# Combination weights turned by four small products, and results stored by transfers that span all 128 partitions

## The chip, the cores and the metric

The kernel runs on one core of one Trainium2 chip. The metric is device time in microseconds (us), the median of several executions. The profile is that of one execution, taken by the hardware profiler. Its engines are TensorE (PE, with its weight loads as PEld), VectorE (DVE), ScalarE (ACT), GpSimd (POOL) and SyncE (SP). SP issues every DMA of this kernel, all on one queue.

## The reference

Eight batches of 576 rows go through attention in chunks of 64 rows, over 8 heads of 64. The result is a matrix x of 4608 rows (tokens) by 512. A soft mixture of experts follows: every token has logits against 32 slots (8 experts with 4 slots each); a softmax over all tokens (`d`) makes the slots' inputs, each expert runs its two matrices on its 4 slots, and a softmax over the 32 slots (`c`) mixes the slots' outputs back into tokens.

```python
# attention, chunk = 64
attn = softmax(scale * q_c @ k_c.T)          # within each chunk of 64 rows
out = attn @ v_c
x = out.transpose(0, 2, 1, 3).reshape(B * S, H * D)       # 4608 x 512
# mixture of experts
logits = x @ phi                             # 4608 x 32
d = softmax(logits, axis=0)
slot_input = (d.T @ x).reshape(E, S_per_e, D)
slot_out[e] = np.maximum(slot_input[e] @ w1[e], 0.0) @ w2[e]
c = softmax(logits, axis=1)
return c @ slot_out                          # 4608 x 512
```

Everything is float32.

## The kernel before

**Tiles of tokens.** The kernel works on nine groups of 512 tokens (index `b`, list `batch`). Eight groups are the first 512 rows of one batch each; the fifth group, at position 4 of the list, collects the last 64 rows of all eight batches. A group is cut into 8 chunks of 64 tokens. Within a group each of four head pairs makes one step, so attention has 36 steps `t`, software pipelined in the loop of lines 427 to 460: `s1` scores, `s2a` transposed weights, `s2b` the product with v, `s3` the transposed x (`xT`), and every fourth step the logits and softmax parts of an earlier group.

**Where a token stands.** `s2b` writes chunk `4m + 2*r2 + c2` (for a normal group: tokens `256m + 128*r2 + 64*c2 + q`, with q from 0 to 63) to partitions `64m + q` of the tile `xb`, at indices `c2` and `r2` of its free dimensions. `s3` (line 261) and `products` (line 361) take the four slices of `xb` that span 128 partitions as `j`, with `c2 = j % 2` and `r2 = j // 2`. One slice thus holds 64 tokens of the group's first half on partitions 0 to 63 and 64 tokens of its second half on partitions 64 to 127.

**Combination weights.** `combination` (lines 338 to 346) leaves the weights `c` of a group in `c_all`, 128 partitions (token within the slice) by 4 slices by 32 slots, the last step being a multiplication on GpSimd. `turn_c` (lines 99 to 103) turns this 128 x 128 block by one TensorE transpose into PSUM and a ScalarE copy back, so that partitions `32j` to `32j+31` hold the 32 slots of slice `j` and the columns its 128 tokens. It is called by `place` for seven groups in the attention loop (at t = 9, 13, ... 33, after `s2a` and before `s1b` and `s2b`), and twice in line 635, between the last `up` of the experts and the last `turn`.

**Weights from memory.** After attention the 16 w1 and 16 w2 blocks of 1 MB each are loaded into the pools `wpa`, `wpb` and the old q/k tiles as these come free (`load_w`, `refill`). All loads have 128 partitions and stand on SP's queue ahead of the stores.

**The last stage.** `down(e, h)` accumulates half h (256 of the 512 columns) of the slots' outputs, `gather` and `spread` copy them to all four row quarters, and `combine(b, h)` (lines 608 to 627) makes the result of group b, half h. For each of the four row quarters one product of 32 rows (`cc[rs]`) gives 128 tokens by 256 columns. Two quarters stand in one PSUM pair and are copied by ScalarE (i = 0) and VectorE (i = 1) into `ob`, 128 partitions by 4 by 256. Then line 627 issues two transfers, one for partitions 0 to 63 and one for 64 to 127: each is 64 partitions by 4 pieces of 1 KB, 256 KB. Two, because the tokens of the upper 64 partitions are not those that follow the lower ones in memory. The order written out by hand in line 643 interleaves the nine `combine(b, 0)` with `down(e, 1)`; the loop of lines 646 and 647 makes the nine `combine(b, 1)`. The tiles `ob` come from the pools of the weights and are separate for each group.

Of the kernel before, what the change touches and what calls it, by code (L numbers as in the profile page):

```python
# [16 lines left out]
def kernel(  # L17
# [10 lines left out]
    nc = tc.nc  # L28
# [3 lines left out]
    B, H, S, D = q.shape  # L32
    P = 128
    CH = 64
# [5 lines left out]
    BT = 4 * P  # L40
# [16 lines left out]
    batch = [0, 1, 2, 3, B] + list(range(4, B))  # L57
# [4 lines left out]
    ident = const.tile([P, P], F32, name="ident")  # L62
# [35 lines left out]

    def turn_c(b, pc):

        cc = c_all[:, 4 * b:4 * b + 4, :].rearrange("p j s -> p (j s)")
        nc.tensor.transpose(out=pc[:, 0:P], in_=cc, identity=ident)
        nc.scalar.copy(cc, pc[:, 0:P])

    with ExitStack() as actx:
# [5 lines left out]
        def bank(name):  # L111
            return ps.tile([P, 512], F32, tag="ps", name=name)

        def pair(name):
            return psp.tile([P, 2, 512], F32, tag="psp", name=name)
# [9 lines left out]
        def tiles(name, shape, which):  # L125
            return {i: ap_.tile([P] + shape, F32, name=f"{name}{i}") for i in which}
# [5 lines left out]
        xb = tiles("x", [2, NHP, 2, P], [1])  # L132
# [124 lines left out]
        def s3(t):  # L257
            px = bank(f"px_{t}")
            n, hp = divmod(t, NHP)
            for j in range(4):  # L260
                nc.tensor.transpose(  # L261
                    out=px[:, P * j:P * (j + 1)], in_=xb[n % 2][:, j % 2, hp, j // 2], identity=ident)
            pv = px.rearrange("p (j x) -> p j x", j=4)
            o = xT[:, :, hp]
            if t == NT - 1 or t % 2 == 0 and t < NT - 6:
                nc.vector.tensor_copy(o, pv)  # L266
            else:
                nc.scalar.copy(o, pv)
# [81 lines left out]
        def partial(b):  # L350
            products(b)
            accumulate(b)

        def products(b):
            eN = lst[b][0]
            pp = pps[b] = bank(f"pp_{b}")
            for j in range(4):
                nc.tensor.matmul(
                    pp[SL * j:SL * (j + 1), :],
                    lhsT=eN[:, j, :],  # L360
                    rhs=xb[b % 2][:, j % 2, :, j // 2],
                    start=True, stop=True,
                )

# [9 lines left out]
        def place(b):  # L374
            turn_c(b, bank(f"pc_{b}"))
# [51 lines left out]
        for t in range(NT - 2):  # L427
# [20 lines left out]
            if t >= 3:  # L448
                s3(t - 3)
# [16 lines left out]
        s1b(t - 1)  # L466
        s1(t)
        s3(t - 4)
        s2b(t - 3)
        load_v(t)  # L470
# [5 lines left out]
        s2b(t - 2)  # L476
        s2a(t)
        s3(t - 3)
        s2b(t - 1)
        natural(NL - 2, False)  # L480
        s2b(t)
        s3(t - 2)
        products(NL - 2)
        s3(t - 1)
        s3(t)
# [122 lines left out]
    def combine(b, h):  # L608
        if h == 0:
            obs[b] = (wpa if b < 7 else wpb).tile([P, 2048], F32, tag="w", name=f"ob_{b}")  # L610
        ob = obs[b].rearrange("p (h j f) -> p h j f", h=2, j=4)[:, h]
        cc = c_all[:, 4 * b:4 * b + 4, :].rearrange("p j s -> p (j s)")
        for i in range(2):
            pf = pair(f"pf_{h}_{b}_{i}")
            for j in range(2):
                rs = slice(SL * (2 * i + j), SL * (2 * i + j + 1))
                nc.tensor.matmul(pf[:, j, 0:DH], lhsT=cc[rs], rhs=sst[h][rs], start=True, stop=True)  # L617
            copy = nc.scalar.copy if i == 0 else nc.vector.tensor_copy
            copy(ob[:, 2 * i:2 * i + 2], pf[:, :, 0:DH])  # L619
        ov = out.rearrange("(b s) f -> b s f", s=S)[..., DH * h:DH * (h + 1)]  # L620
        for x in range(2):

            if batch[b] < B:
                o = ov[batch[b], 4 * CH * x:4 * CH * (x + 1)].rearrange("(j q) f -> q j f", j=4)
            else:
                o = ov[4 * x:4 * x + 4, BT:S].rearrange("j q f -> q j f")
            nc.sync.dma_start(o, ob[CH * x:CH * (x + 1)])

    hrs = {}
    for e in range(0, E, 2):  # L630
# [3 lines left out]
    for b in (NL - 2, NL - 1):  # L634
        turn_c(b, bank(f"pc_{b}"))
# [4 lines left out]


    steps = {"d": lambda e: down(e, 1), "c": lambda b: combine(b, 0), "g": gather, "s": spread}
    order = "s0 d0 c0 c1 d1 c2 d2 c3 d3 c4 d4 c5 d5 c6 d6 c7 d7 g1 c8 s1"
    for x in order.split():
        steps[x[0]](int(x[1:]))
    for b in range(NL):
        combine(b, 1)
# [30 lines left out]
```

## Time and profile before

| | |
|---|---|
| time, median of 3 runs | 256.41 us (256.22 to 256.86) |
| time of the profiled execution | 255.84 us |
| its span in the trace | 254.0 us |
| mean granted TensorE clock | 0.968 |
| PE busy | 214.0 us (84%) |
| DVE busy | 158.7 us (63%) |
| ACT busy | 144.4 us (57%) |
| POOL busy | 6.8 us (3%) |
| bytes read from and written to memory | 61.93 MB, 9.44 MB |
| packets of the one DMA queue | 89168, 98.0% of 16 engines' span |

The span is the time from the first to the last event that the trace shows; the execution takes 1.8 us more. The profile's page cuts the span into 40 slices of 6.35 us and gives for each how busy the engines were, in tenths. The chain of waits follows the work that ended last back from the end. Other views give, for one source line, the durations of its instructions (lowest, median, highest, in ns) and the time from a DMA's issue to its landing (in us), or, for stretches of time, the busy time of the engines and what the DMA engines moved.

### The profile page before, as it was taken

Reading aid. Unit: us, or ns where it says so; the run is one execution under the profiler, and the core shown is the slowest. Engines: PE = TensorE matmul, PEld = TensorE weight load, DVE = VectorE, ACT = ScalarE, POOL = GpSimd, SP = SyncE. Lnnn points to the kernel's source line nnn. Section 1 sums busy time; section 2 is a strip of 40 time slices with the busy share of each in tenths; the row PEclk is TensorE's granted clock in tenths of the full one; section 3 lists DMA queues with packets and bytes.
Section 4 is the critical chain, followed back from the end, with each engine's and each line's share of the span. In section 5 each row is a group of like instructions: output and inputs, shape, how many; then the busy total and the mean of one; then the engine's idle time right before and its main releaser. Section 6 shows DMA issues by size and latency. Waiting matters only on the chain.

```text
span 254.0 us, 7973 instructions
## 1 busy us (share of the span) xinstructions
PE 214.0 (84%) x3262; PEld 150.0 (59%) x3262; DVE 158.7 (63%) x356; ACT 144.4 (57%) x291; POOL 6.8 (3%) x29
## 2 busy tenths in 40 slices
PE   6888988998998998998998998989899998988000
PEld 3667876875885785875776776676533453445000
DVE  4578786986985985985985985985630102456100
ACT  2697868758758757867767776775221202345000
POOL 1000000000000000000000000000040000000000
PEclk9999999999999999999999999999999999999755
DMA  6999999999999899999999788986999999999996
GB/s 193 335 293 268 318 337 295 277 273 244 257 269 199 264 317 243 308 322 341 290 308 300 217 242 227 354 215 230 320 331 346 348 348 347 321 254 258 275 254 183
DMA packets 89203, 71.88 MB, mean 283 GB/s; under 512 B 41040, under 2 KB 85072, under 8 KB 89168
## 3 DMA queue, kind: packets, MB, share of 16 engines
q1 hardware_dynamic: 89168, 71.38, 98.0%
q8 instruction: 26, 0.43, 0.7%
q14 instruction: 9, 0.07, 0.1%
HBM read 61.93 MB, written 9.44 MB: 281 GB/s over the span
## 4 chain that ended last, share of the span: by engine, by line
PE 46%; DVE 22%; ACT 19%; issue 4%; DMA 1%; POOL 0%; ACTq 0%; DVEq 0%
ACT qkT L188 15%; PE pqk L173 7%; PE po L583 6%; DVE qkT L186 6%; PE psc L200 6%; PE ph L551 6%; DVE x L250 5%; PE pav L241 5%; PE px L261 4%; PE pf L617 4%; PE pt L223 3%; DVE xT L266 3%; DVE sc L210 2%; DVE mx L208 1%; DVE rc L249 1%
## 5 line engine op out<-in xcount | busy, mean ns | idle before, releaser
L188 ACT COPY qkT<-pqk 64x512 f32<-64x512 f32 x107 | 66.7, 624 | 29.8 <-PE pqk L173 28.1
L173 PE MATMUL pqk<-ident,qk_w 128*128 128x128 f32 x288 | 40.4, 284 | 5.4 <-DVE qkT L186 4.7
L186 DVE COPY qkT<-pqk 64x512 f32<-64x512 f32 x37 | 25.8, 696 | 23.3 <-ACT qkT L188 19.8
L200 PE MATMUL psc<-qkT 128*64 128x128 f32 x576 | 39.4, 279 | 1.0 <-DVE qkT L186 1.0
L173 PEld LDWEIGHTS pqk<-ident,qk_w 128*128 128x128 f32 x288 | 31.6, 143 | 14.3 <-DVE qkT L186 7.0
L200 PEld LDWEIGHTS psc<-qkT 128*64 128x64 f32 x576 | 30.7, 137 | 4.0 <-ACT qkT L188 1.2
L261 PE MATMUL px<-ident,x 128*128 128x128 f32 x144 | 22.7, 282 | 5.6 <-DVE x L250 4.9
L210 DVE TENSOR_TENSOR sc<-psc,mx 128x512 f32<-128x512 f32 x36 | 24.9, 691 | 1.3
L250 DVE TENSOR_TENSOR x<-pav,rc 128x512 f32<-128x512 f32 x36 | 24.9, 691 | 1.2
L261 PEld LDWEIGHTS px<-ident,x 128*128 128x128 f32 x144 | 15.6, 141 | 16.6 <-DVE x L250 11.8
L241 PE MATMUL pav<-v,at 64*64 64x65 f32 x1152 | 25.1, 224 | 0.3 <-ACT eN L324 0.3
L208 DVE TENSOR_REDUCE mx<-psc 128x8 f32<-128x512 f32 x36 | 24.4, 677 | 0.5 <-PE psc L200 0.4
L223 PE MATMUL pt<-ident,sc 128*128 128x128 f32 x144 | 22.1, 275 | 2.8 <-ACT sc L215 1.6
L241 PEld LDWEIGHTS pav<-v,at 64*64 64x64 f32 x1152 | 20.1, 134 | 5.8 <-issue 3.7
L215 ACT ACTIVATE sc<-sc 128x512 f32<-128x512 f32 x36 | 23.1, 642 | 0.1
L225 ACT COPY at<-pt 128x512 f32<-128x512 f32 x36 | 21.2, 588 | 1.9 <-PE pt L223 1.5
L619 DVE COPY ob<-pf 128x512 f32<-128x512 f32 x18 | 12.2, 689 | 12.7 <-PE pf L617 12.7
L223 PEld LDWEIGHTS pt<-ident,sc 128*128 128x128 f32 x144 | 16.6, 141 | 3.9 <-ACT sc L215 2.3
L619 ACT COPY ob<-pf 128x512 f32<-128x512 f32 x18 | 10.3, 586 | 13.0 <-PE pf L617 12.0
L617 PE MATMUL pf<-sst,c_all 32*128 32x256 f32 x144 | 14.3, 423 | 1.6 <-ACT ob L619 0.5
L551 PE MATMUL ph<-w,siT 128*32 128x512 f32 x128 | 14.6, 596 | 0.1
L583 PE MATMUL po<-w,hz 128*32 128x256 f32 x224 | 14.3, 383 | 0.1
(86 smaller groups left out, 172.9 us busy)
## 6 DMA issues: line engine op xcount, KB each, us to landing
w<-in_moe_w_dram SPq DMA_DIRECT2D x30, 1024.0 KB, 7.3
out_dram<-ob SPq DMA_DIRECT2D x36, 256.0 KB, 4.3
qk_w<-in_k_dram SPq DMA_DIRECT2D x32, 256.0 KB, 5.7
qk_w<-in_q_dram SPq DMA_DIRECT2D x32, 256.0 KB, 5.8
v<-in_v_dram SPq DMA_DIRECT2D x64, 128.0 KB, 5.0
qk_w<-in_moe_w_dram SPq DMA_DIRECT2D x2, 1024.0 KB, 7.6
qk_w<-in_k_dram SPq DMA_DIRECT2D x8, 128.0 KB, 5.5
qk_w<-in_q_dram SPq DMA_DIRECT2D x8, 128.0 KB, 5.2
```

What stands on the lines that cost most here:

```text
L173: nc.tensor.transpose(out=pt[:, 1 - isq, o:o + P], in_=src[:, a, P * i:P * (i + 1)], identity=ident)
L186: nc.vector.tensor_copy(o, pv[D * j:D * (j + 1), a])
L188: nc.scalar.copy(o, pv[D * j:D * (j + 1), a])
L200: nc.tensor.matmul(pv[CH * r2:CH * (r2 + 1), m, c2], lhsT=qT[:, o:o + CH], rhs=kb[:, :, o:o + CH], start=True, stop=True,)
L208: nc.vector.reduce_max(mx, pv, axis=AX.X)
L210: nc.vector.tensor_tensor(sc.rearrange("p (r x) -> p r x", x=CH), pv, mx.unsqueeze(2).to_broadcast([P, 8, CH]), ALU.subtract)
L223: nc.tensor.transpose(out=pt[:, P * r:P * (r + 1)], in_=sc[:, r], identity=ident)
L241: nc.tensor.matmul(pav[CH * m:CH * (m + 1), c2, i * VW:(i + 1) * VW], lhsT=at[rs, 2 * m + a, r2, :], rhs=v_sb[t % NV][rs, 2 * m + r2, a, : ...
L250: nc.vector.tensor_tensor(xb[n % 2][:, :, hp].rearrange("p c m (a d) -> p c (m a) d", a=2), av[..., 0:D], rc.to_broadcast([P, 2, 4, D]), A ...
L261: nc.tensor.transpose(out=px[:, P * j:P * (j + 1)], in_=xb[n % 2][:, j % 2, hp, j // 2], identity=ident)
L551: nc.tensor.matmul(ph[SL * i:SL * (i + 1), :], lhsT=siT[:, j, :], rhs=wt[1, e, j // 2][:, j % 2, DM * h:DM * (h + 1)], start=(j == 0), sto ...
L583: nc.tensor.matmul(po[h][SL * c:SL * (c + 1), :], lhsT=hzs[e][:, 2 * c + b, :], rhs=w[:, 2 * c + b, :], start=(e == 0 and b == 0), stop=(e ...
```

## The change

```diff
     def turn_c(b, pc):
         cc = c_all[:, 4 * b:4 * b + 4, :].rearrange("p j s -> p (j s)")
-        nc.tensor.transpose(out=pc[:, 0:P], in_=cc, identity=ident)
+        for c2 in range(2):
+            for x in range(2):
+                rs = slice(CH * x, CH * (x + 1))
+                nc.tensor.matmul(pc[rs, CH * c2:CH * (c2 + 1)], lhsT=cc[rs, CH * c2:CH * (c2 + 1)],
+                                 rhs=ident[rs, rs], start=True, stop=True)
         nc.scalar.copy(cc, pc[:, 0:P])
...
-                    out=px[:, P * j:P * (j + 1)], in_=xb[n % 2][:, j % 2, hp, j // 2], identity=ident)
+                    out=px[:, P * j:P * (j + 1)], in_=xb[n % 2][:, j // 2, hp, j % 2], identity=ident)
...
-                    rhs=xb[b % 2][:, j % 2, :, j // 2],
+                    rhs=xb[b % 2][:, j // 2, :, j % 2],
...
-        for x in range(2):
-
-            if batch[b] < B:
-                o = ov[batch[b], 4 * CH * x:4 * CH * (x + 1)].rearrange("(j q) f -> q j f", j=4)
-            else:
-                o = ov[4 * x:4 * x + 4, BT:S].rearrange("j q f -> q j f")
-            nc.sync.dma_start(o, ob[CH * x:CH * (x + 1)])
+        if batch[b] < B:
+            nc.sync.dma_start(ov[batch[b], 0:BT].rearrange("(j p) f -> p j f", j=4), ob)
+        else:
+            for c2 in range(2):
+                nc.sync.dma_start(ov[c2::2, BT:S].rearrange("j q f -> q j f"), ob[CH * c2:CH * (c2 + 1)])
```

The slices `j` are numbered the other way (`c2 = j // 2`, `r2 = j % 2`). `turn_c` makes four products of a 64 x 64 block with a 64 x 64 identity in place of the transpose of the whole block: each 64 x 64 block is turned, and it stays in its half of the partitions, while a transpose of the whole moves the two off-diagonal blocks across. The row quarter `2x + j % 2` then holds 128 tokens that follow each other, `128 * quarter + column`. So in a normal group the partitions of `ob` are tokens in the order of memory, and `combine` stores its 512 KB by one transfer of 128 partitions by 4 pieces of 1 KB. The collected group, whose chunks come from eight batches, is still stored by two transfers of 64 partitions. In place of 36 transfers of 256 KB there are 16 of 512 KB and 4 of 256 KB.

## The prediction

> **What bounds the kernel now.** I read the page's slices first, for where the compute engines stop.
>
> ```profile
> span 254.0 us, 7973 instructions
> ...
> PE   6888988998998998998998998989899998988000
> PEld 3667876875885785875776776676533453445000
> DVE  4578786986985985985985985985630102456100
> ACT  2697868758758757867767776775221202345000
> ...
> DMA  6999999999999899999999788986999999999996
> GB/s 193 335 293 268 318 337 295 277 273 244 257 269 199 264 317 243 308 322 341 290 308 300 217 242 227 354 215 230 320 331 346 348 348 347 321 254 258 275 254 183
> ```
>
> In the last three slices (19 us) no compute engine does anything, while the DMA engines are busy to the end. The chain of waits agrees: its last piece is a copy of the last results.
>
> ```profile
> 234.84 1.29 DVE ob L619 x2
> ```
>
> It ends at 236.1; the remaining 17.9 us are stores that are still flowing. So the second view is the busy time by stretches (columns: length; PE, PEld, DVE, ACT, POOL busy; granted clock, DMA share, GB/s).
>
> ```profile
> 208.00:214.00 6.00, 5.00 (x62) 2.46 (x54) 1.12 (x2) 1.41 (x3) 0.00 (x0) 1.00 1.09 348
> 216.00:218.00 2.00, 2.00 (x36) 0.92 (x36) 1.01 (x2) 0.94 (x2) 0.00 (x0) 1.00 1.07 342
> 218.00:220.00 2.00, 2.00 (x36) 0.84 (x28) 1.05 (x2) 0.80 (x2) 0.00 (x0) 1.00 1.06 341
> 220.00:222.00 2.00, 2.00 (x35) 0.92 (x32) 0.71 (x2) 0.59 (x1) 0.00 (x0) 1.00 0.95 283
> 222.00:226.00 4.00, 4.00 (x57) 1.80 (x56) 1.90 (x4) 1.32 (x3) 0.00 (x0) 1.00 0.93 258
> 226.00:236.00 10.00, 8.00 (x74) 4.40 (x73) 6.41 (x10) 5.98 (x11) 0.00 (x0) 1.00 0.93 261
> 236.00:246.00 10.00, 0.00 (x0) 0.00 (x0) 0.13 (x1) 0.00 (x0) 0.00 (x0) 0.59 0.92 260
> 246.00:252.00 6.00, 0.00 (x0) 0.00 (x0) 0.00 (x0) 0.00 (x0) 0.00 (x0) 0.50 0.89 255
> 252.00:254.00 2.00, 0.00 (x0) 0.00 (x0) 0.00 (x0) 0.00 (x0) 0.00 (x0) 0.50 0.09 29
> ```
>
> To 214 the queue carries weight loads of 128 partitions, at 348 GB/s. From 222 it carries stores alone, at 255 to 261, with the engines still 0.89 to 0.93 busy. Loads and stores both move pieces of 1 KB. So the bound from about 217 on is the store stream, and it runs at three quarters of the rate just shown by the same engines. From 220 to the end the rows add up to 2·283 + 4·258 + 10·261 + 10·260 + 6·255 + 2·29 = 8396 KB. At about 255 the last row holds 0.2 us of flow, so 8396 KB take 32.2 us, 261 GB/s.
>
> **Why it is slow.** The third view is that of the storing line and of the two lines that load v, the second of them for the collected group.
>
> ```profile
> L627 SPq DMA_DIRECT2D out_dram<-ob x36: 595/931/1307, 213.8 to 248.8; - x36
> ...
> DMA to landing us min/median/max: 3.7/4.3/5.5
> ...
> L162 SPq DMA_DIRECT2D v<-in_v_dram x16: 595/607/868, 72.5 to 92.8; - x16
> ...
> DMA to landing us min/median/max: 3.9/6.0/8.2
> ...
> L157 SPq DMA_DIRECT2D v<-in_v_dram x64: 367/458/1618, 2.8 to 165.9; - x64
> ...
> DMA to landing us min/median/max: 2.3/5.0/7.1
> ```
>
> Line 162 moves 64 KB to 64 partitions, line 157 128 KB to 128 partitions, in the same pieces. With half the bytes the 64-partition transfer costs SP more (595 against 367 ns at best) and lands later (3.9 against 2.3 us at best, 6.0 against 5.0 in the median). So transfers of half the partitions are the slow kind also as loads, and writing memory is not needed for it. (The comparison isn't clean: the sources of line 162 lie further apart.) The stores are this kind: their quickest issue takes the same 595 ns.
>
> [...]
>
> **The change, part by part.**
>
> *Stores.* 32 of the 36 transfers become 16 of 512 KB from 128 partitions; the collected group's 4 stay. Both halves waited for the same two copies before, so nothing is issued later than now. SP's 36 issues lie end to end (36.25 us from 213.8 to the end of the last):
>
> ```profile
> 203.83 5.71 SPq L95 DMA_DIRECT2D w<-in_moe_w_dram  x2
> 213.78 36.25 SPq L627 DMA_DIRECT2D out_dram<-ob  x36
> ```
>
> so either SP paces the stream or the engines push back on it; both ways are eased. 20 issues at the 931 ns median would be 18.6 us, at the 458 ns of line 157, which has as many pieces for each transfer, 9.2 us. Either is under the time the bytes need. If an issue grew with its pieces to 2 x 931 ns, SP would again set the pace: a rival below.
>
> The rate after isn't in the trace, since no store has 128 partitions. Lower bound: 255 GB/s, today's. Upper bound: short stretches of mixed loads run higher than 348, as the slices of the stretch from 72 to 95 us (0.575 us each) show:
>
> ```profile
> GB/s 130 100 349 335 378 328 386 362 304 175 131 183 181 249 221 183 86 194 138 147 55 126 21 406 370 385 435 344 372 347 249 231 210 306 378 370 374 372 378 315
> ```
>
> some 375 held for 3 us. I take 345, between the loads of 128 partitions in the same pieces (348) and the best stretch that is mostly stores (341). The 8396 KB take 24.3 us in place of 32.2: **-7.9 us**.
>
> *What is late next.* Would the results come in time? The copies of the first half end at about 213.7 and then every 1.64 us, to 226.6; the second half's first group ends at 228.5, the last at 236.1.
>
> ```profile
> 225.91 0.69 DVE L619 COPY ob<-pf 128x512 f32<-128x512 f32 x1 [0.18 <-PE pf L617]
> ...
> 227.70 1.07 ACT L619 COPY ob<-pf 128x512 f32<-128x512 f32 x2 [0.80 <-PE pf L617]
> 227.76 0.69 DVE L619 COPY ob<-pf 128x512 f32<-128x512 f32 x1 [1.16 <-PE pf L617]
> ```
>
> At 345 GB/s one 512 KB transfer takes 1.52 us. The stores begin to flow at 217.0: 9.44 MB of stores less 8.40 MB are 1.04 MB before 220, 3.0 us at 341. Then group k of the first half starts at 217.0 + 1.52k, the first of the second half at 230.7. Its copies end at 228.5; with some 2 us from issue to flow (an estimate: the 2.3 us best landing of line 157 less its own 0.4) it is there at 230.4, just in time. The end of 244.3 lies 8 us behind the last copy, so the queue stays the bound. Only much over 345 GB/s would the first half run dry: at 375 the second half starts at 230.4 and the nine end at 243.0, a gain of 9.2; without any limit of the queue the last copy's 236.1 and a landing of 3.7 give 239.8, a gain of 12.4.
>
> *Turning.* Nine transposes go, 36 products come. Row of the transposes, row of the products of this shape (64x64 against 65 columns), and one step's 32 of them:
>
> ```profile
> L102 PE MATMUL pc<-ident,c_all 128*128 128x128 f32 x9 | 2.9, 320 | 0.7 <-ACT hr L562 0.3
> ...
> L241 PE MATMUL pav<-v,at 64*64 64x65 f32 x1152 | 25.1, 224 | 0.3 <-ACT eN L324 0.3
> ...
> 48.38 0.70 PE L241 MATMUL pav<-v,at 64*64 64x65 f32 x32
> ```
>
> A float32 product leaves two records (16 products a step, 32 records), so a turn has 8. At best, overlapped as in line 241, they take 0.70·8/32 = 0.18 us, below the transpose's 0.32; in a row 8·0.224 = 1.79, 1.47 more. The nearest row is the overlapped one with a lead of one product, about 0.35 us. For the seven turns in attention, which no idle PE hides in full, and the two that stand ahead of `down`, I take +0.2 us in all; bounds -1.2 and +13.2. The copy behind it keeps its shape.
>
> *Numbering of the slices.* Lines 261 and 361 read the same shapes with the same partitions in another order: 0.
>
> **Sum.** On the profiled execution: 255.8 - 7.9 + 0.2 = 248.1 us. The median of the runs is 0.6 above the profiled one (256.4 against 255.8), so 256.4 - 7.7 = **248.7 us**. At 341 and 348 GB/s it is 249.0 and 248.5.
>
> **Rivals.**
>
> - *Half the way.* Another limit, such as memory's writing or the last halves of the collected group, holds the stream near 300 GB/s: 28.0 us in place of 32.2, 252.4. For it: 341 was seen for only some 4 us, with a backlog and the end of the loads beside it. Against: 341 is still a stretch in which most bytes are stores.
> - *No gain.* The store stream is limited by bytes or pieces written, not by its shape: 261 GB/s stay, 256.6 with the turns. A doubled issue (2 x 931 ns for 512 KB, 282 GB/s) would give 29.8 us and 254.2, near it. [...] Against it speak the rows of lines 157 and 162.
> - *Slower.* The four products run one behind the other where PE sets the pace, in the turn between transposes and line 241: 1.47 us each, 13.2 for nine, 256.4 - 7.9 + 13.2 = 261.7. It decides from 0.9 us a turn (7.9/9), and sooner if the stores gain less. Against it stands the row of 32 records in 0.70 us.
> - *It does not do what it says.* The bytes and the piece size (1 KB) stay; only if the transfer were spread over fewer engines than now would it fail; this would be the second rival's number or worse.
>
> **How the numbers follow.** Forecast (330 GB/s or more, 246 to 250 us): 0.66. Half the way (250 to 254): 0.17. No gain: 0.11, which is within 0.3%, about what a measurement of this kernel can tell from no change. Slower: 0.06. Faster 0.83, same 0.11, slower 0.06. Failing to do what it says is within no gain. The range begins at 246.0, between the 247.4 of 375 GB/s and the 244.2 of a queue without limit, and ends at 253.5 (some 275 to 280 GB/s); it leaves out the worst of half the way, no gain and slower, and holds 0.66 and some 0.14.
>
> **What would show it.** The GB/s of the stretches behind 220 rise to 330 or more; the span's end lies 8 to 9 us behind the last copy, not 18; issues of 512 KB take under 1.5 us of SP; copies end at 236 as now, a few tenths later if the turns cost; the group of the turn shows 8 records in some 0.35 us. Wrong would be: 260 GB/s again (no gain), or copies that end over 1 us later (turns on the path).

## The result and the profile after

| | before | changed |
|---|---|---|
| median | 256.63 us (256.22 to 257.39, 4 runs) | 249.18 us (249.11 to 250.24, 4 runs) |
| profiled execution: span | 254.0 us | 247.4 us |
| mean granted TensorE clock | 0.968 | 0.985 |

The ratio is 0.9716, 95% interval 0.968 to 0.9751: faster by 2.8%. The forecast was 248.7 us, with a range from 246.0 to 253.5. An execution that was longer at a lower granted clock (one of 251.47 us, in the repeat of the changed kernel below) is left out of its run's median. The mean clock differs by the tail: in both kernels it is 1.00 in the last stretches in which PE works and down to 0.50 in those behind them, of which the kernel before has more.

The page of the changed kernel, its span and the slices of PE and of the DMA engines (now 6.2 us each):

```profile
span 247.4 us, 8098 instructions
...
PE   6989889998999999899898899898989999899820
...
DMA  6999999979999999999999976997799999999996
GB/s 183 324 300 256 323 313 268 305 226 288 291 190 286 212 319 278 290 325 288 325 309 255 323 232 178 289 331 201 243 354 345 345 348 348 348 368 326 347 306 232
```

The stretch in which the compute engines stand still while stores flow is shorter: one slice without PE and one with two tenths of it, in place of three without. The view by stretches (length; PE, PEld, DVE, ACT, POOL busy; clock, DMA share, GB/s) shows where the time went:

```profile
216.00:222.00 6.00, 6.00 (x92) 2.66 (x88) 2.14 (x4) 1.82 (x4) 0.00 (x0) 1.00 1.09 373
222.00:226.00 4.00, 4.00 (x64) 1.72 (x56) 2.08 (x3) 1.70 (x3) 0.00 (x0) 1.00 1.02 293
226.00:236.00 10.00, 8.61 (x84) 4.90 (x82) 5.90 (x10) 5.55 (x10) 0.00 (x0) 1.00 1.05 354
236.00:240.00 4.00, 0.42 (x4) 0.02 (x2) 1.16 (x2) 0.59 (x1) 0.00 (x0) 0.99 0.98 282
240.00:245.00 5.00, 0.00 (x0) 0.00 (x0) 0.00 (x0) 0.00 (x0) 0.00 (x0) 0.50 1.04 348
```

The stores now flow at 348 to 373 GB/s where they flowed at 255 to 261, but for two dips to 293 and 282. The view of the two storing lines says what stands there: line 627 is the transfer of 128 partitions, line 630 that of 64 partitions, by which the collected group is still stored, twice for each half of the columns.

```profile
L627 SPq DMA_DIRECT2D out_dram<-ob x16: 372/470/1797, 214.8 to 240.9; - x16
...
L630 SPq DMA_DIRECT2D out_dram<-ob x4: 666/1070/1331, 221.1 to 235.0; - x4
```

SP issues the first pair of line 630 from 221.1 to 222.7 and the second from 233.7 to 236.4: each just ahead of a dip. An issue of 512 KB takes SP 470 ns in the median, one of 256 KB from 64 adjacent partitions 1070.

One thing went the other way. The timeline gives the last copies (first two lines: the changed kernel's last copies; the copies of before ended at 236.1) and the first maximum of the scores, from the changed kernel and from the one before:

```profile
235.87 1.29 DVE L624 COPY ob<-pf 128x512 f32<-128x512 f32 x2 [0.63 <-PE pf L622]
236.04 0.59 ACT L624 COPY ob<-pf 128x512 f32<-128x512 f32 x1 [0.37 <-PE pf L622]
```
```profile
11.44 0.69 DVE L213 TENSOR_REDUCE mx<-psc 128x8 f32<-128x512 f32 x1
```
```profile
10.21 0.69 DVE L208 TENSOR_REDUCE mx<-psc 128x8 f32<-128x512 f32 x1
```

The copies end at 237.2, 1.0 us later than before. But the first scores, long before any turn, are already 1.2 us later. So of 254.0 - 247.4 = 6.6 us, the last stage gives 7.6 (span behind the last copy: 17.9 before, 10.2 now) and the later copies take 1.0 back.

### The profile page after: what moved, and what is told of

It is laid out like the page before. It is cut to its first block, busy times and chain, and to the rows that moved or that the text cites. A ratio compares the mean times of both kernels' runs of the same rounds, so it can differ in the third digit from the quotient of the medians.

```text
span 247.4 us, 8098 instructions
## 1 busy us (share of the span) xinstructions
PE 215.5 (87%) x3325; PEld 152.4 (62%) x3325; DVE 159.0 (64%) x356; ACT 144.5 (58%) x291; POOL 6.8 (3%) x29
## 4 chain that ended last, share of the span: by engine, by line
PE 43%; DVE 28%; ACT 18%; issue 4%; DMA 2%; POOL 0%; SPq 0%; ACTq 0%; DVEq 0%; POOLq 0%
ACT qkT L193 14%; DVE qkT L191 6%; PE po L588 6%; PE ph L556 6%; DVE x L255 6%; PE pqk L178 6%; PE psc L205 5%; PE pf L622 4%; PE pav L246 4%; PE px L266 4%; DVE xT L271 3%; PE pt L228 3%; DVE mx L213 2%; DVE sc L215 2%; DMA qk_w<-in_k_dram 2%
## 5 line engine op out<-in xcount | busy, mean ns | idle before, releaser
L178 PE MATMUL pqk<-ident,qk_w 128*128 128x128 f32 x288 | 41.5, 289 | 7.1 <-DVE qkT L191 5.2
L178 PEld LDWEIGHTS pqk<-ident,qk_w 128*128 128x128 f32 x288 | 32.5, 146 | 16.1 <-DVE qkT L191 7.6
L205 PE MATMUL psc<-qkT 128*64 128x128 f32 x576 | 40.3, 283 | 0.0
L205 PEld LDWEIGHTS psc<-qkT 128*64 128x64 f32 x576 | 31.4, 139 | 3.0 <-issue 0.8
```

What stands on the lines that cost most here:

```text
L178: nc.tensor.transpose(out=pt[:, 1 - isq, o:o + P], in_=src[:, a, P * i:P * (i + 1)], identity=ident)
L205: nc.tensor.matmul(pv[CH * r2:CH * (r2 + 1), m, c2], lhsT=qT[:, o:o + CH], rhs=kb[:, :, o:o + CH], start=True, stop=True,)
```

## The experiments

Theory (span): a transfer of 64 adjacent partitions is the slow kind, and one whose partitions are spread over all 128 the fast one. Rivals: the number of transfers, with SP's issue as the pace; the turns or the numbering; 64 partitions as such.

**Halves again, with the new turn.**

```diff
-            nc.sync.dma_start(ov[batch[b], 0:BT].rearrange("(j p) f -> p j f", j=4), ob)
+            o = ov[batch[b], 0:BT].rearrange("(j p) f -> p j f", j=4)
+            for x in range(2):
+                nc.sync.dma_start(o[CH * x:CH * (x + 1)], ob[CH * x:CH * (x + 1)])
```

> The changed kernel (new turn, new numbering), but each normal group is stored again by two transfers of 64 adjacent partitions, 256 KB each. Span theory (transfers of 64 adjacent partitions are the slow kind, those that span all 128 the fast one): the store stream falls back to 255 to 265 GB/s, 256.5 us (255.5 to 257.5), as before the change; this also prices the turns, since only they and the numbering then differ from the kernel before: within 0.3 us of it. Count theory (what counts is the number of transfers, SP's issue being the pace): also 256.5. Rival that the turn or the numbering bring part of the gain: under 255.0.

Measured: 255.79 us, ratio to before 0.9983 (0.9956 to 1.001). Its stretches:

```profile
222.00:226.00 4.00, 4.00 (x54) 1.76 (x50) 2.26 (x4) 1.69 (x3) 0.00 (x0) 1.00 0.93 260
226.00:236.00 10.00, 7.64 (x73) 4.31 (x72) 6.17 (x10) 5.61 (x11) 0.00 (x0) 1.00 0.94 263
```

The whole gain goes with the store, and with it the old 260 GB/s come back. The turns and the numbering alone change nothing that can be told from noise: by the interval between 1.1 us less and 0.3 more, where within 0.3 was expected.

**All partitions, but as many transfers as before.**

```diff
+            for i in range(2):
+                nc.sync.dma_start(o[:, 2 * i:2 * i + 2], ob[:, 2 * i:2 * i + 2])
```

> The changed kernel, but each normal group is stored by two transfers of 128 partitions by 2 pieces (two row quarters each), 256 KB each: 36 transfers as before the change, all partitions as after it. Span theory: 340 GB/s or more, 249.2 us (248.5 to 250.5). Count theory: SP issues 36 times, some 0.9 us each, the stream stays at 255 to 270 GB/s, 255 to 257 us.

Measured: 248.5 us, ratio 0.9719 (0.9674 to 0.9765), as fast as the changed kernel. The line of its 32 transfers, and two stretches:

```profile
L629 SPq DMA_DIRECT2D out_dram<-ob x32: 372/670/1398, 213.6 to 242.3; - x32
```
```profile
216.00:222.00 6.00, 6.00 (x92) 2.67 (x96) 2.77 (x4) 2.35 (x4) 0.00 (x0) 1.00 1.09 373
...
226.00:236.00 10.00, 8.04 (x74) 4.43 (x74) 6.40 (x10) 6.02 (x11) 0.00 (x0) 1.00 1.05 347
```

The same 256 KB, the same pieces, the same number of transfers as before, at 347 to 373 GB/s, but for dips (304 from 222 to 226, 277 from 236 to 240) behind the collected group's transfers, as in the changed kernel. Number and size of the transfers are out, and so is SP's count of issues as the pace. That the long issues of before came from the DMA engines pushing back is argued, from two things: the quickest of them took no longer than those of spread transfers (595 ns, beside 600 in the next run), and each byte took more of the engines' time (a share of 0.93 at 261 GB/s from 226 to 236, in place of 1.05 at 347: some 18% more).

**64 partitions, but every second one.**

```diff
+            for x in range(2):
+                nc.sync.dma_start(o[x::2], ob[x::2])
```

> The changed kernel, but each normal group is stored by two transfers of 64 partitions, the even ones and the odd ones, 256 KB each. Span theory, if it is the spread over the 128 partitions that counts: 249.5 us (248.5 to 251). If 64 partitions are slow however they are spread, or the number of transfers counts: 255 to 257. Between: part of each.

Measured: 249.29 us, ratio 0.9745 (0.9689 to 0.9801).

```profile
L629 SPq DMA_DIRECT2D out_dram<-ob x32: 600/634/1507, 214.9 to 243.8; - x32
...
DMA to landing us min/median/max: 3.0/3.3/5.1
```
```profile
226.00:236.00 10.00, 8.61 (x88) 4.84 (x82) 5.88 (x11) 5.54 (x10) 0.00 (x0) 1.00 1.00 332
```

64 partitions are not slow in themselves. An issue still costs SP 600 ns at best, as in the kernel before (595), but the median falls from 931 ns before to 634 and the landing from 4.3 us to 3.3. What counted was that the 64 were adjacent. (In memory these transfers write every second row, too, where the halves write 64 rows on end; the run without a new turn, further below, parts the two.)

**The old turn with the large transfer.** The kernel before, with line 627 replaced by the changed kernel's store of the normal groups.

```diff
-            if batch[b] < B:
-                o = ov[batch[b], 4 * CH * x:4 * CH * (x + 1)].rearrange("(j q) f -> q j f", j=4)
...
+        if batch[b] < B:
+            nc.sync.dma_start(ov[batch[b], 0:BT].rearrange("(j p) f -> p j f", j=4), ob)
```

> The kernel before with its transpose and numbering, and the stores of the normal groups alone changed: one transfer of 128 partitions by 4 pieces, so that 384 of each normal group's 512 rows land in another order within their batch. Theory that the gain is all of the store: 249.0 us (248.5 to 249.7), the changed kernel's less at most 0.3 for the turns. Rival that the nine turns cost 1 us (the copies of the changed profile end 1.0 us later than before): 248.2 or less, with copies that end at 236.1. Rival that the turn brings part of the gain: 250 or more.

Measured: 248.22 us, ratio 0.9701 (0.9647 to 0.9754), and 249.18 and (in the next run) 248.87 with the new turn. The time misses the 248.5 to 249.7 that was expected and fits the rival's "248.2 or less"; but the intervals of the ratios overlap, so the times can't part the turns from nothing. What speaks against the rival is that its copies do not end at 236.1: the first scores come at 11.4 us and the copies end at 237.2, late as in the changed profile, without one of the new products.

**The changed kernel again, beside the next two.**

> The changed kernel once more, to stand beside the next two on the same chip: 249.2 us (248.0 to 250.2). Theory that the copies end 1.0 us later in its profile because of the turns: first scores at 10.2 us after the span's start as in the profile before, copies end a microsecond later all the same. Theory that the microsecond comes from the start (first scores at 11.4 in the changed profile against 10.2 before, and it varied from 10.1 to 11.4 in the other runs without regard to the turn): the copies end 225.8 us (within 0.2) behind the first scores, as in all others.

Measured: 248.87 us (247.41 to 249.86, 5 runs), ratio 0.9723 (0.9675 to 0.9772). First scores at 11.1, last copies at 238.2: 227.1 us between them, not the 225.8 expected. So the expectation fails as it was put: the same program took 225.7 us from first scores to last copy in one execution and 227.1 in the other. The timelines of all runs say where. The scores of step 9 are the last before the first turn, those of step 35 the last of attention, with all seven turns of the loop between them; two rows of the kernel before, then two of this run:

```profile
47.42 0.66 DVE L208 TENSOR_REDUCE mx<-psc 128x8 f32<-128x512 f32 x1
...
168.86 0.69 DVE L208 TENSOR_REDUCE mx<-psc 128x8 f32<-128x512 f32 x1 [0.36 <-PE psc L200]
```
```profile
49.74 0.66 DVE L213 TENSOR_REDUCE mx<-psc 128x8 f32<-128x512 f32 x1
...
171.08 0.69 DVE L213 TENSOR_REDUCE mx<-psc 128x8 f32<-128x512 f32 x1 [0.36 <-PE psc L205]
```

| start of scores, us | turn | step 0 | step 9 | step 35 | 9 to 35 |
|---|---|---|---|---|---|
| before | old | 10.21 | 47.42 | 168.86 | 121.44 |
| old turn with the large transfer | old | 11.41 | 48.52 | 169.91 | 121.39 |
| changed | new | 11.44 | 48.69 | 170.05 | 121.36 |
| halves again | new | 10.26 | 47.40 | 168.67 | 121.27 |
| quarters | new | 10.09 | 47.48 | 169.08 | 121.60 |
| every second | new | 10.85 | 48.91 | 170.12 | 121.21 |
| changed again | new | 11.12 | 49.74 | 171.08 | 121.34 |

The stretch with the turns is as long with the old as with the new, within 0.25 us. What varies, from 47.4 to 49.7 us for the same work, is the time to step 9, ahead of every turn. Both the 1.0 us of the changed profile and the 2.1 of this one arose there. (The next run has 122.4 from 9 to 35: one step without a turn, 19 to 20, took 8.4 us there and 7.4 to 7.6 in the others. The runs behind it have 121.3 to 121.6, but for the one with the turns five times over.)

**What the collected group's transfers cost.** Its results go to other rows by one transfer:

```diff
-            for c2 in range(2):
-                nc.sync.dma_start(ov[c2::2, BT:S].rearrange("j q f -> q j f"), ob[CH * c2:CH * (c2 + 1)])
+            nc.sync.dma_start(ov[0, CH:S].rearrange("(j p) f -> p j f", j=4), ob)
```

> The changed kernel, but the collected group too is stored by one transfer of 128 partitions, to rows 64 to 575 of the first batch, so that these rows are written twice and the last 64 rows of the batches are not all written. It prices the four transfers of 64 adjacent partitions that the changed kernel still has. Span theory: the dips to 293 GB/s (222 to 226) and 282 (236 to 240) go, 350 or more there, 1.3 to 1.7 us off: 247.7 us, ratio to the changed kernel 0.994. If the dips come from something else in these stretches (the change from the first half of the columns to the second, the end of the weight loads): 249.2, the dips stay.

Measured: 247.98 us, ratio 0.9688 (0.9645 to 0.973), beside 0.9723 for the changed kernel. The stretches of the two dips, and then the dips of the changed kernel's repeat, whose transfers of 64 partitions came over 1 us later than in its first profile:

```profile
222.00:226.00 4.00, 4.00 (x64) 1.77 (x56) 1.52 (x3) 1.17 (x2) 0.00 (x0) 1.00 1.09 384
...
236.00:240.00 4.00, 1.42 (x14) 0.77 (x12) 1.61 (x3) 1.32 (x3) 0.00 (x0) 1.00 1.03 337
```
```profile
224.00:226.00 2.00, 2.00 (x32) 0.91 (x32) 0.69 (x1) 0.58 (x1) 0.00 (x0) 1.00 1.02 305
...
238.00:240.00 2.00, 0.00 (x0) 0.00 (x0) 0.18 (x1) 0.00 (x0) 0.00 (x0) 1.00 1.00 280
```

384 and 337 GB/s, in place of 293 and 282 in the first profile and of 305 and 280 in the repeat: the dips were the four transfers of adjacent halves. The time falls by 0.9 us, less than the 1.3 to 1.7 expected, and the intervals overlap: part of what the dips cost is lost again between them (338 GB/s from 226 to 236, where the changed kernel had 354).

**The collected group on alternate partitions.** The copy behind its turn writes the columns alternately, so that its halves are the even and the odd partitions, all rows where they belong:

```diff
+            nc.scalar.copy(cc.rearrange("p (q c) -> p c q", c=2), pc[:, 0:P].rearrange("p (c q) -> p c q", c=2))
...
-                nc.sync.dma_start(ov[c2::2, BT:S].rearrange("j q f -> q j f"), ob[CH * c2:CH * (c2 + 1)])
+                nc.sync.dma_start(ov[c2::2, BT:S].rearrange("j q f -> q j f"), ob[c2::2])
```

> The changed kernel, but the copy behind the turn of the collected group writes the columns so that its even partitions hold four batches' tokens and its odd ones the other four's, and its two transfers take every second partition: same number of transfers, same bytes, all rows where they belong. Span theory: as when its rows land elsewhere, 247.7 us (247.0 to 248.3), the dips gone; the strided copy costs some tenths at most, hidden, since the end is the queue's. If 64 partitions are slow in themselves: 249.2.

Measured: 247.67 us (246.56 to 248.18, 6 runs), ratio 0.9671 (0.9627 to 0.9715).

```profile
222.00:226.00 4.00, 4.00 (x64) 1.77 (x56) 1.74 (x4) 1.22 (x3) 0.00 (x0) 1.00 1.06 354
...
236.00:240.00 4.00, 0.00 (x0) 0.00 (x0) 0.68 (x2) 0.14 (x1) 0.00 (x0) 0.83 1.04 340
```

The dips are gone here too. It has the lowest median of all runs, 1.2 us under the changed kernel beside it; the two ratios' intervals overlap, so the step is likely and not settled.

**Two queues.**

```diff
-            nc.sync.dma_start(o, ob[CH * x:CH * (x + 1)])
+            (nc.scalar if x else nc.sync).dma_start(o, ob[CH * x:CH * (x + 1)])
```

> The kernel before with the transfers of the upper 64 partitions issued by ACT, those of the lower by SP. Span theory: SP's issue is not the pace, nothing changes but how halves meet: 256.4 us (254.5 to 257.5), 255 to 275 GB/s. If SP's 36 issues of some 0.95 us are the pace: 18 on each, the stream goes to 340 GB/s, 249 to 250 us. A mean of the two if two queues make lower and upper halves run beside each other: 250 to 254.

Measured: 252.62 us, ratio 0.9862 (0.9814 to 0.9911), between the two. Two lines of its timeline say why it can't be read further:

```profile
240.25 0.59 ACT L619 COPY ob<-pf 128x512 f32<-128x512 f32 x1 [1.43 <-DVE ob L619]
...
242.27 0.58 ACT L619 COPY ob<-pf 128x512 f32<-128x512 f32 x1 [1.43 <-DVE ob L619]
```

ACT's issue waits for VectorE's copy, and ACT's next copy stands behind the issue: a new loop of 2.0 us a group, so the copies, not the stores, set the end (the last of them ends at 245.6). The first stretches (340 GB/s from 216 to 222, 307 from 222 to 226) would fit halves that run beside each other better, but that stays open.

**No new turn at all.** The kernel before; the copy behind its transpose alternates the columns of every group, and the 36 transfers take every second partition.

```diff
         nc.tensor.transpose(out=pc[:, 0:P], in_=cc, identity=ident)
-        nc.scalar.copy(cc, pc[:, 0:P])
+        nc.scalar.copy(cc.rearrange("p (q m) -> p m q", m=2), pc[:, 0:P].rearrange("p (m q) -> p m q", m=2))
...
-            nc.sync.dma_start(o, ob[CH * x:CH * (x + 1)])
+            nc.sync.dma_start(o, ob[x::2])
```

> The kernel before with its transpose and its numbering; only the copy behind the transpose writes the columns alternately, so that the two halves of a group's tokens stand on the even and the odd partitions, and each of the 36 transfers of 256 KB takes every second partition. All rows land where they belong. Span theory: the four products and the one large transfer are not needed for the gain, 248.0 us (247.0 to 249.3), stretches of stores at 330 to 370 GB/s without dips. Theory that the number of transfers or 64 partitions hold the stream: 255 to 257. If the spread gains less where every transfer has it: 250 to 253.

Measured: 248.25 us, ratio 0.9695 (0.9666 to 0.9724): the whole gain with one transpose, 36 transfers and a strided copy. Each transfer writes the same rows of memory, in the same pieces, as in the kernel before; only the partitions that it reads are others. So it is the partitions, and not the order of the rows in memory.

```profile
226.00:236.00 10.00, 8.61 (x86) 4.92 (x82) 6.03 (x10) 5.64 (x11) 0.00 (x0) 1.00 0.98 327
236.00:240.00 4.00, 0.29 (x4) 0.00 (x0) 1.03 (x2) 0.49 (x1) 0.00 (x0) 0.91 1.04 346
```
```profile
234.00:235.00 1.00, 0.91 (x14) 0.31 (x6) 0.73 (x2) 0.63 (x2) 0.00 (x0) 1.00 0.56 184
```

From 240 to 245 it has 340 GB/s, from 222 to 226 331. The expectation of 330 or more without dips fails in one stretch: from 234 to 235 the DMA share falls to 0.56, with 1.03 in the microsecond after it, right behind an issue that took SP 1.47 us (232.8 to 234.3). Why that issue took so long isn't shown.

**Turns five times over.**

```diff
-        for c2 in range(2):
+        for c2 in 5 * [0, 1]:
```

> The changed kernel with the four products of each turn made five times over (20 products, 40 records). It prices a turn. Theory that the products overlap as in the attention product and the turns cost nothing that shows: 36 records more of PE at some 22 ns, 0.7 us a turn, 6.3 for nine, of which those at places where PE waits anyway cost nothing: 250 to 255.5 us, that is 0.1 to 0.7 us a turn for four times its work, under 0.2 for once. Rival that they run one behind the other: 32 records more at 0.22 us, 7 us a turn, 63 us for nine: over 290 us.

Measured: 255.94 us, ratio 1.0012 (0.9976 to 1.0047). That is 6.8 to 7.1 us over the changed kernel for 36 extra sets of four products, above the 6.3 expected at most: 0.19 to 0.20 us a set. Its scores of steps 9 and 35 give a price in which the stores of the results have no part:

```profile
48.36 0.66 DVE L213 TENSOR_REDUCE mx<-psc 128x8 f32<-128x512 f32 x1
...
175.56 0.69 DVE L213 TENSOR_REDUCE mx<-psc 128x8 f32<-128x512 f32 x1
```

From 9 to 35 it takes 127.2 us in place of 121.4, 5.8 more for the 28 extra sets of seven turns: 0.21 us a set, near the overlapped rate (0.18 us) and far from the 1.79 of products one behind the other. So nine turns once over are worth some 1.9 us of PE at this price, and the nine transposes that they replace, 0.32 us each by their row, 2.9 us at most.

## Why the prediction was right

**The bound.** Right: the store stream set the end, and it alone gave the gain (halves again: 0.9983).

**Its cause.** Right in direction, too wide in words. The step called transfers of half the partitions the slow kind; every second partition showed that half the partitions are fast if they are spread (332 GB/s from 226 to 236 and a median landing of 3.3 us, in place of 261 and 4.3), and the run without a new turn that the rows of memory have no part in it (327 GB/s there, ratio 0.9695). The rows of the v loads that the step rested on were of adjacent halves, and couldn't tell this. Why a transfer from adjacent partitions is the slower one, no trace shows.

**The stores: -7.9 us.** 7.6 in the profiled execution, reckoned behind the last copy. The 345 GB/s stood for two things that the step didn't part: 348 to 373 for the new transfers, and the dips of the four old ones, 0.9 to 1.2 us by the runs that removed them. That the two nearly cancel is luck: from 220 to the end of the flow at 245.3 the mean is 334 (384 from 220 to 222, the rows above, and 0.12 MB behind 245). The highest stretch above is 384, and the longest ones of spread stores have 327 to 354.

**The 341 GB/s between 218 and 220.** A weak row. The kernel with halves again has the same transfers and 292 there:

```profile
218.00:220.00 2.00, 2.00 (x34) 0.93 (x32) 0.70 (x2) 0.59 (x1) 0.00 (x0) 1.00 0.98 292
```

It served as a lower anchor for the rate, where 348 alone would have done.

**The turns: +0.2 us, bounds -1.2 and 13.2.** Right within what was left open; nothing of it shows (121.4 us with seven turns, old or new). The profile lets one look at one turn among its neighbours, in the kernel before and then in the changed one:

```profile
48.12 0.33 PE L102 MATMUL pc<-ident,c_all 128*128 128x128 f32 x1
...
48.38 0.70 PE L241 MATMUL pav<-v,at 64*64 64x65 f32 x32
```
```profile
49.38 0.38 PE L106 MATMUL pc<-ident,c_all 64*64 64x64 f32 x5
49.55 0.27 PE L246 MATMUL pav<-v,at 64*64 64x65 f32 x1
49.55 0.22 PE L106 MATMUL pc<-ident,c_all 64*64 64x64 f32 x1
...
49.66 0.64 PE L246 MATMUL pav<-v,at 64*64 64x65 f32 x30
```

The four products, 0.45 us of PE for a turn (4.0 us for nine) against the 0.35 forecast, overlap with the products of line 246, which have the same shape; from the turn's start to the end of those products it is 0.96 us before and 0.92 now.

**What would show it.** The dips missed the 330 GB/s. The end lies 10.2 us behind the last copy, not 8 to 9; but there the sign was at odds with its own sum, which gives 17.9 - 7.9 = 10.0 (the 8 were reckoned to the end of the flow, which in the kernel before came 1.8 us ahead of the span's end). One issue took 1.8 us of SP, not under 1.5. And the sign named for turns on the path, copies over 1 us later, came about at 1.0 with another cause: it should have been measured from the last event ahead of the first turn, not from the span's start.

**The rivals.** No gain: refuted by all of the spread transfers. Half the way: the dips were its one part, "the last halves of the collected group", at about a third of the price or less (0.9 to 1.2 us, against the 3.7 that part that rival from the forecast). Slower by turns in a row: refuted by the turns five times over. That SP's issue grows with its pieces: 470 ns for 512 pieces, refuted.

## What to carry to other kernels

Look at the compute engines' last busy slice before anything else: where DMA goes on alone behind it, as here for 17.9 us, only the stream's GB/s count, to be compared with the best that the same pieces reach elsewhere in the trace. If a stream of stores from 64 adjacent partitions sets the end (here at 255 to 263 GB/s), spread each store: over all 128 partitions (354 GB/s from 226 to 236), or over every second one (327 to 332), which a strided copy ahead of it can arrange, with no change of number or size (the run without a new turn, 0.9695). (For loads no run here tried it.) And judge a stage by its distance from the last event that the change couldn't touch: here the start alone varied by up to 2.3 us.

## What the runs showed of the hardware that had not been expected

- Transfers of 64 partitions bring the gain of the large ones when they take every second partition (249.29 and 248.25 us; 332 and 327 GB/s from 226 to 236, where the changed kernel had 354; 346 and 340 in the last stretches of the second), though their issue costs SP 600 ns at best, where one of 128 partitions costs 372 with as many or twice as many pieces.
- Spread stores run for some microseconds faster than the loads in the same pieces: 373 from 216 to 222 in the changed kernel and 384 from 222 to 226 with the collected group elsewhere, against 348 GB/s from 208 to 214 before.
- Products of 64 x 64 blocks beside others of their shape cost PE some 0.2 us for four, less than the one transpose of 128 x 128 that they replace shows (0.32).
- The same work up to step 9 took 47.4 to 49.7 us in different executions, while the 26 steps behind it took 121.2 to 121.6 in all of the table.
